# Transposed scores of two batches in one visit of four banks, in the last attention step of a fused cross-attention and gated feed-forward kernel

## The chip, the cores and the metric

The kernel runs on one core of one Trainium2 chip. The metric is the device time of one execution, in microseconds; lower is better. A core has a TensorE for matmuls (PE in the profile, with its weight loads as PEld), a VectorE (DVE), a ScalarE (ACT), a GpSimd (POOL) and a SyncE (SP), which issues most of the transfers. TensorE writes into PSUM; the kernel's four pools there have eight banks together, and a bank takes a tile of 128x512 numbers in f32.

## The reference

For each of 8 batches and 8 heads there are 512 tokens `x` and 32 state rows, of width 64. Tokens read the state, state rows read the tokens; the two results, put under each other (544 rows a batch, 512 columns), go through a gated feed-forward.

```python
scores = scale * np.matmul(x, state.transpose(0, 1, 3, 2))
a = exp(scores - scores.max(-1)); a /= a.sum(-1)
xread = np.matmul(a, state)
scores2 = scale * np.matmul(state, x.transpose(0, 1, 3, 2))   # the transposed scores
a2 = exp(scores2 - scores2.max(-1)); a2 /= a2.sum(-1)
sread = np.matmul(a2, x)
x2 = concatenate([xread, sread], axis=2)   # then heads side by side: 4352 x 512
out = ((1 / (1 + exp(-(x2 @ w_gate)))) * (x2 @ w_val)) @ w_out   # d_ff = 1536
```

## The kernel before

Everything is issued in an order written out by hand; each engine works through its own list in that order, and a scheduler adds the waits.

**Steps.** After a start written out call by call, a loop runs over `b` from 2 to 8. A step has 12 turns, `f` from 0 to 11, one for each 128 columns of `d_ff`. A turn does `gv_mm(b, f)`, the gate and value matmuls of the tokens of batch `b` (two PSUM tiles of the pool `GV`, which has two banks), `gv_th` (the tanh, on ACT), `gv_glu` (the product with the value, on DVE) and `out_mm(b - 1, f)`, four matmuls of the output of the batch before. In step 7 the output matmuls stand first in a turn. Turn by turn `out_mm` fills one bank (pool `OU`, one buffer), for four matmuls in each of three turns; in the third turn ACT copies the bank out (`res`, L318), and the next group's first matmul has to wait for that copy. Step 8 is the feed-forward of the state rows of all batches, which are gathered in `XS`; step 7 is the last step with attention in it.

**Transposed scores.** For one batch they go through these functions: `cT_mm` makes them in two PSUM banks (`e` = 0 and 1, each with four heads) with eight matmuls on 64x32 parts of TensorE, each 512 columns wide; `cT_max(b, e)` takes a maximum per row and scales it into the bias `nb` (DVE, L188 and L190); `cT_exp(b, e)` is the exponential with its sum (ACT, L196); `cT_nrm(b, e)` takes the reciprocal of the sum (DVE, L201) and multiplies by it on POOL (L204); `c_dma(b)` transposes the result through two transfers of SP's queue into the tile `Eb`; `sr_mm` multiplies it with the tokens (16 matmuls, 64 columns wide, L216); and `sr_cp` copies both halves of that into `XS` (ACT, then DVE, L221). Of the tiles `cE` (the exponentials), `nb` and `Eb` there are two buffers each.

**The last attention step.** Batches 0 and 1, whose feed-forward was done in the start, have their transposed scores only in step 7, beside the feed-forward of batch 7: `col(0, t)` in turns 0 to 4, `col(1, t)` in turns 3 to 7, `sr_mm` of batch 0 in turn 8, of batch 7 in turn 9 (its copies in turn 10), of batch 1 in turn 11. All of these take banks of the pool `SWP`, which has four; in step 7 nothing else uses it. The bank of the pool `AT` is idle in this step.

Of the kernel before, what the change touches and what calls it, by code (L numbers as in the profile page):

```python
# [16 lines left out]
def kernel(  # L17
# [14 lines left out]
    nc = tc.nc  # L32
    B, H, S, D = x.shape
# [30 lines left out]
    AT, OU, GV, SWP = (p_at, "at"), (p_out, "outp"), (p_gv, "gv"), (p_sw, "swp")  # L64
    xfs, xbs, xTs = {}, {}, {}
    Es, E1s, Ebs, abs_, aTs, SWs, glus = {}, {}, {}, {}, {}, {}, {}
    vec, act, pool = nc.vector.tensor_copy, nc.scalar.copy, nc.gpsimd.tensor_copy
# [42 lines left out]
    def at_xT_dma(b):  # L110
        xT = xT_tile(b)
        for c in range(4):
            nc.sync.dma_start_transpose(xT[:, :, c], xbs[b][:, c].rearrange("p h d -> p (h d)"))

    def S_mm(b, i, place, jjs=(0, 1)):
        if jjs[0] == 0:
            held["S", b, i] = place[0].tile((128, 4, 2, 2, Ns), FP, name="Sp", tag=place[1])
        ps = held["S", b, i]
        for jj in jjs:
            for c in range(4):  # L120
                nc.tensor.matmul(ps[:, c, :, jj], xTs[b][:, 2 * i + jj, c], sTz[:, b, 2 * i + jj], start=True, stop=True)  # L121

    def S_max(b, i):

        if b not in E1s:
            E1s[b] = ap_.tile((128, 4, 2, 4, Ns), FP, name="E1")
        ps = held["S", b, i].rearrange("p c e j n -> p (c e) j n")
        mx = held["mx", b, i] = ap_.tile((128, 8, 2), FP, name="mx")
        nc.vector.tensor_reduce(mx, ps, AX.X, ALU.max)  # L129

    def S_sub(b, i):

        mx, ps = held["mx", b, i], held["S", b, i].rearrange("p c e j n -> p (c e) j n")
        nc.vector.tensor_tensor(halfE(b, i), ps, mx.unsqueeze(3).to_broadcast((128, 8, 2, Ns)), ALU.subtract)  # L134

    def S_exp(b, i):
        nc.scalar.activation(halfE(b, i), halfE(b, i), AF.Exp, scale=scale)  # L137
# [4 lines left out]
    def n_sum(b, i):  # L142
        rs = ap_.tile((128, 8, 2), FP, name="rs")
        nc.vector.tensor_reduce(rs, halfE(b, i), AX.X, ALU.add)  # L144
        ri = held["ri", b, i] = ap_.tile((128, 8, 2), FP, name="ri")
        nc.vector.reciprocal(ri, rs)  # L146

    def n_mul(b, i, eng, lo=0, n=4):
        if b not in abs_:
            abs_[b] = ap_.tile((128, 4, 2, 128), BF, name="ab")  # L150
        ri, ce = held["ri", b, i], slice(2 * lo, 2 * lo + 2 * n)
        eng.tensor_tensor(abs_[b].rearrange("p c e (j n) -> p (c e) j n", n=Ns)[:, ce, 2 * i:2 * i + 2],  # L152
                          halfE(b, i)[:, ce], ri[:, ce].unsqueeze(3).to_broadcast((128, 2 * n, 2, Ns)), ALU.mult)
# [17 lines left out]
    def aT_dma(b):  # L171
        for c in range(4):
            nc.sync.dma_start_transpose(aT_tile(b)[:, c], abs_[b][:, c].rearrange("p e k -> p (e k)"))

    def cT_mm(b, places):

        pss = [p[0].tile((128, 512), FP, name="cTp", tag=p[1]) for p in places]
        for j in range(4):
            for e in range(2):
                rows = slice(e * 64, (e + 1) * 64)  # L180
                nc.tensor.matmul(pss[e][j * Ns:(j + 1) * Ns], sTz[rows, b, j, e],  # L181
                                 xTs[b][rows, j].rearrange("p c t -> p (c t)"), start=True, stop=True)
        held["cT", b] = pss

    def cT_max(b, e):

        mx = ap_.tile((128, 1), FP, name="cm")
        nc.vector.tensor_reduce(mx, held["cT", b][e], AX.X, ALU.max)  # L188
        nb = held["nb", b, e] = ap_.tile((128, 1), FP, name="nb")
        nc.vector.tensor_scalar(nb, mx, -scale, None, op0=ALU.mult)  # L190

    def cT_exp(b, e):

        ex = held["cE", b, e] = ap_.tile((128, 512), FP, name="cE")
        cs = held["cs", b, e] = ap_.tile((128, 1), FP, name="cs")
        nc.scalar.activation(ex, held["cT", b][e], AF.Exp, bias=held["nb", b, e], scale=scale, accum_out=cs)  # L196

    def cT_nrm(b, e, eng):

        rc = ap_.tile((128, 1), FP, name="rc")  # L200
        nc.vector.reciprocal(rc, held["cs", b, e])  # L201
        if ("cN", b) not in held:
            held["cN", b] = ap_.tile((128, 2, 512), BF, name="cN")
        eng.tensor_scalar(held["cN", b][:, e], held["cE", b, e], rc, None, op0=ALU.mult)  # L204

    def c_dma(b):
        Ebs[b] = ap_.tile((128, 4, 2, 128), BF, name="Eb")
        for e in range(2):
            nc.sync.dma_start_transpose(Ebs[b][:, :, e], held["cN", b][:, e])

    def sr_mm(b, place):
        sr = held["sr", b] = place[0].tile((128, 4, 2, Ns), FP, name="srp", tag=place[1])
        Eb = Ebs[b].rearrange("p c e (j n) -> p c e j n", n=Ns)
        for j in range(4):
            for c in range(4):
                nc.tensor.matmul(sr[:, j], xbs[b][:, c, 2 * j:2 * j + 2].rearrange("p h d -> p (h d)"),  # L216
                                 Eb[:, c, :, j], start=(c == 0), stop=(c == 3))

    def sr_cp(b, e, cp):
        rows = slice(e * 64, (e + 1) * 64)  # L220
        cp(XS[rows, :, b * Ns:(b + 1) * Ns], held["sr", b][rows, :, e])  # L221
# [46 lines left out]
    def sw_cp(b, lo, w, e, cp):  # L268
        cp(*sw_left.pop((b, lo, w, e)))  # L269
# [115 lines left out]
    def col(b, t):  # L385

        if t == 0:
            cT_mm(b, (AT, SWP) if b > 1 else (SWP, SWP))
            cT_max(b, 0)
        elif t == 1:  # L390
            cT_max(b, 1)
            cT_exp(b, 0)
        elif t == 2:
            cT_exp(b, 1)
        elif t == 3:
            cT_nrm(b, 0, nc.gpsimd)
        else:
            cT_nrm(b, 1, nc.gpsimd)
            c_dma(b)

    def row(b, t):

        if t == 0:
            S_mm(b, 0, AT)
            S_max(b, 0)
        elif t == 1:
            S_sub(b, 0)
            S_mm(b, 1, SWP)
            S_max(b, 1)
        elif t == 2:  # L410
            S_sub(b, 1)
            S_exp(b, 0)
        elif t == 3:
            S_exp(b, 1)
            n_sum(b, 0)
            n_mul(b, 0, nc.gpsimd)
        elif t == 4:
            n_sum(b, 1)
            n_mul(b, 1, nc.gpsimd)
        else:  # L420
            aT_dma(b)
# [274 lines left out]
    for b in range(2, B + 1):  # L696
        nb = b + 1 if b + 1 < B else None
        for f in range(NF):

            v, q = divmod(f, 6)  # L700
            if nb is not None and q == 0:
                sw_wide(nb, v)
                sw_cp(nb, v, 0, 0, act)
                sw_cp(nb, v, 0, 1, act)
            ahead = nb is not None and q == 0
            for first in (ahead, not ahead):
                if first:
                    gv_mm(b, f, SWP if b == B and f % 2 else GV)
                    gv_th(b, f)
                    gv_glu(b, f)  # L710
                elif b < B or f < 9:
                    out_mm(b - 1, f)
            if nb is not None:
                if q == 0:
                    sw_cp(nb, v, 1, 0, vec)
                if q in (1, 3, 4):
                    k = max(q + 1, 3)
                    sw_cp(nb, v, k // 2, k % 2, act)
                if f == 10:
                    sr_cp(b, 0, act)  # L720
                    sr_cp(b, 1, vec)
                if 0 <= f - (b < 4) < 6:
                    row(nb, f - (b < 4))
                elif f >= 7:
                    col(nb, f - 7)
                if f == (6 if b > 3 else 3) and nb + 2 < B:
                    load_x(nb + 2, nc.sync, 4 if nb + 3 == B else 1)
                if f == (1 if b > 2 else 6) and nb + 1 < B:
                    cast_x(nb + 1, pool, 0, 4)
                    cast_x(nb + 1, pool, 4, 4)  # L730
                    at_xT_dma(nb + 1)
            if b < B and f == 9:
                sr_mm(b, SWP)
            if b == B - 1:
                if f == 10:
                    sr_cp(b, 0, act)
                    sr_cp(b, 1, vec)
                for k in range(2):
                    if 0 <= f - 3 * k < 5:
                        col(k, f - 3 * k)  # L740
                    elif f == 8 + 3 * k:
                        sr_mm(k, SWP)
                        sr_cp(k, 0, act)
                        sr_cp(k, 1, vec)
    for k in range(6):
        out_mm(B, k)
    out_last(B - 1, 3)
# [30 lines left out]
```

## Time and profile before

| | |
|---|---|
| median of 3 runs | 230.65 us (230.24 to 230.70) |
| the profiled execution | 230.65 us, of which the profile's span is 228.9 us |
| clock that TensorE was granted | 1.0 of full speed |
| busy, share of the span | PE 96%, ACT 63%, DVE 60%, POOL 31% |
| chain that ended last, by engine | PE 84%, DMA 7%, ACT 2%, POOL 2% |
| step 7, from its first output matmul to the first of step 8 | 176.16 to 199.55 us |

The span is cut by instructions: each row of the timeline gives a start, a duration, the engine, the line, what is written from what, and in brackets the idle time before it and what ended it. Durations of pipelined instructions overlap: four matmuls of 512 columns show 1.03 us, but the next group starts 0.86 us after them. In this text "tanh of turn 3" and the like are those of step 7.

### The profile page before, as it was taken

The numbers are of one execution on the slowest core, as the hardware profiler recorded it, in microseconds if no ns is written. First come the engines' busy times: TensorE is split into PE (matmuls) and PEld (weight loads), VectorE is DVE, ScalarE is ACT, GpSimd is POOL, SyncE is SP. The second block draws the span as 40 slices with busy tenths as digits, with TensorE's granted clock in tenths as the row PEclk, the third lists the DMA queues.
The fourth block names the chain that finished last, engine by engine and source line by source line (L and its number), as shares of the span: only waits on it lengthen the run. The fifth ranks groups of instructions, "written<-read, shape, count | busy, mean of one in ns | idle before, by whom it ended". The sixth has DMA issues, their size and how long they took to land.

```text
span 228.9 us, 5007 instructions
## 1 busy us (share of the span) xinstructions
PE 219.1 (96%) x1885; PEld 111.5 (49%) x1911; DVE 138.0 (60%) x266; ACT 143.1 (63%) x288; POOL 71.4 (31%) x77
## 2 busy tenths in 40 slices
PE   8868999999999999999999999999999999999994
PEld 7653444434444444444444444445444434566744
DVE  0889779766587557666766577648755664422311
ACT  3588787677575866676767767584857655422411
POOL 3986371240507080307130533031301355000001
PEclk9999999999999999999999999999999999999999
DMA  6999979935794374842443766313121312411114
GB/s 215 269 201 285 206 88 182 269 85 126 209 292 134 61 181 94 246 148 74 92 126 83 238 84 142 89 46 87 57 46 75 99 37 69 116 39 77 46 26 115
DMA packets 47271, 29.49 MB, mean 129 GB/s; under 512 B 29872, under 2 KB 42544, under 8 KB 47248
## 3 DMA queue, kind: packets, MB, share of 16 engines
q1 hardware_dynamic: 40096, 21.84, 36.5%
q0 software_dynamic: 6864, 7.14, 17.0%
q8 instruction: 15, 0.25, 0.4%
q10 hardware_dynamic: 288, 0.20, 0.3%
q14 instruction: 8, 0.07, 0.1%
HBM read 18.35 MB, written 8.91 MB: 119 GB/s over the span
## 4 chain that ended last, share of the span: by engine, by line
PE 84%; DMA 7%; ACT 2%; issue 2%; POOL 2%; SPq 1%; DVE 0%; ACTq 0%
PE outp L314 36%; PE gvp L283 34%; PE swp L231 5%; PE gvp L286 5%; DMA wg<-in_moe_w_gate_dram 4%; DMA xf<-in_x_dram 2%; PE srp L216 2%; PE Sp L121 1%; SPq L74 1%; PE outp L334 1%; PE cTp L181 1%; POOL cN L204 1%; ACT res L318 1%; POOL xb L91 1%; ACT SW L269 1%
## 5 line engine op out<-in xcount | busy, mean ns | idle before, releaser
L298 DVE SCALAR_TENSOR_TENSOR glu<-th,gvp 128x512 bf16<-128x512 f32 (+1 forms) x108 | 70.3, 656 | 69.1 <-ACT th L293 52.8
L314 PE MATMUL outp<-wo,glu 128*128 128x512 bf16 x370 | 95.5, 379 | 1.7 <-issue 0.3
L283 PE MATMUL gvp<-aT,SW 128*128 128x512 bf16 x384 | 96.6, 379 | 0.3 <-DVE aT L169 0.3
L293 ACT ACTIVATE th<-gvp 128x512 f32<-128x512 f32 (+1 forms) x108 | 61.8, 576 | 51.2 <-PE gvp L283 41.4
L283 PEld LDWEIGHTS <-SW 128*128 128x128 bf16 x384 | 36.3, 98 | 44.8 <-issue 3.1
L314 PEld LDWEIGHTS <-glu 128*128 128x128 bf16 x396 | 36.5, 98 | 40.8 <-issue 3.2
L204 POOL TENSOR_SCALAR cN<-cE,rc 128x512 bf16<-128x512 f32 x16 | 24.9, 1564 | 66.2 <-DVE rc L201 53.4
L269 ACT CAST SW<-swp 128x512 bf16<-128x512 f32 x74 | 41.0, 586 | 3.5 <-PE swp L231 2.5
L152 POOL TENSOR_TENSOR ab<-E,ri 128x512 bf16<-128x512 f32 x16 | 16.7, 1047 | 48.4 <-DVE ri L146 21.7
L318 ACT ACTIVATE res<-outp 128x512 f32<-128x512 f32 x33 | 19.7, 597 | 16.8 <-PE outp L314 16.6
L269 DVE CAST SW<-swp 128x512 bf16<-128x512 f32 x22 | 14.7, 681 | 1.0 <-PE swp L231 1.0
L91 POOL CAST xb<-xf 128x1024 bf16<-128x1024 f32 (+1 forms) x14 | 13.6, 986 | 4.9 <-DMA xf<-in_x_dram 4.9
L196 ACT ACTIVATE cE<-cTp,nb 128x512 f32<-128x512 f32 x16 | 11.1, 694 | 0.8 <-POOL cN L204 0.8
L144 DVE TENSOR_REDUCE rs<-E 128x16 f32<-128x512 f32 x16 | 10.8, 675 | 0.7 <-ACT E L137 0.7
L188 DVE TENSOR_REDUCE cm<-cTp 128x1 f32<-128x512 f32 x16 | 10.9, 682 | 0.4 <-PE cTp L181 0.4
L137 ACT ACTIVATE E<-E 128x512 f32<-128x512 f32 x16 | 10.1, 637 | 1.6 <-DVE E L134 1.6
L129 DVE TENSOR_REDUCE mx<-Sp 128x16 f32<-128x512 f32 x16 | 10.7, 674 | 0.4 <-PE Sp L121 0.4
L134 DVE TENSOR_TENSOR E<-Sp,mx 128x512 f32<-128x512 f32 x16 | 10.9, 684 | 0.1
L325 POOL DMA_DIRECT2D out_dram<-res x2 | 1.1, 550 | 30.1 <-ACT res L318 30.1
L231 PE MATMUL swp<-wg,sTc 64*32 64x512 bf16 (+1 forms) x192 | 8.4, 328 | 0.2
L348 PE MATMUL warm<-ones 128*128 128x128 bf16 x87 | 7.6, 256 | 1.0 <-DVE ones L429 1.0
L231 PEld LDWEIGHTS <-sTc 64*32 64x32 bf16 x384 | 4.8, 91 | 7.4 <-issue 4.7
(62 smaller groups left out, 134.2 us busy)
## 6 DMA issues: line engine op xcount, KB each, us to landing
out_dram<-res SPq DMA_DIRECT2D x31, 256.0 KB, 2.4
xf<-in_x_dram SPq DMA_DIRECT2D x12, 256.0 KB, 4.8
xf<-in_x_dram SPq DMA_DIRECT2D x3, 1024.0 KB, 6.3
wo<-in_moe_w_out_dram POOLq DMA_DIRECT2D x3, 512.0 KB, 8.9
wv<-in_moe_w_val_dram POOLq DMA_DIRECT2D x2, 512.0 KB, 9.1
wg<-in_moe_w_gate_dram POOLq DMA_DIRECT2D x2, 512.0 KB, 10.1
xf<-in_x_dram POOLq DMA_DIRECT2D x2, 512.0 KB, 8.0
xf<-in_x_dram POOLq DMA_DIRECT2D x1, 1024.0 KB, 12.8
```

Of the source, the lines that this page charges most:

```text
L91: cp(xbs[b].rearrange("p c h d -> p h c d")[:, lo:lo + n], xfs[b][:, lo:lo + n])
L152: eng.tensor_tensor(abs_[b].rearrange("p c e (j n) -> p (c e) j n", n=Ns)[:, ce, 2 * i:2 * i + 2], halfE(b, i)[:, ce], ri[:, ce].unsqueeze ...
L196: nc.scalar.activation(ex, held["cT", b][e], AF.Exp, bias=held["nb", b, e], scale=scale, accum_out=cs)
L204: eng.tensor_scalar(held["cN", b][:, e], held["cE", b, e], rc, None, op0=ALU.mult)
L231: nc.tensor.matmul(pss[e][j * Ns:(j + 1) * Ns, o:o + n], sTc[rows, b, j] if b > 1 else sTz[rows, b, j, e], (wg, wv)[w][rows, j, lo:lo + n] ...
L269: cp(*sw_left.pop((b, lo, w, e)))
L283: nc.tensor.matmul(ps, SWs[b][:, g, w, fs], aTs[b][:, :, g], start=(g == 0), stop=(g == 1))
L286: nc.tensor.matmul(ps, (wg, wv)[w][:, j, fs], XS[:, j], start=(j == 0), stop=(j == 3))
L293: nc.scalar.activation(th, held["gv", b, f][0], AF.Tanh, scale=0.5)
L298: nc.vector.scalar_tensor_tensor(glus[b][:, f], held["th", b, f], 1.0, held["gv", b, f][1], ALU.add, ALU.mult)
L314: nc.tensor.matmul(ops[b, c], glus[b][:, f, c * 128:(c + 1) * 128], wo[:, f], start=(f == 0), stop=(f == NF - 1))
L318: nc.scalar.activation(res, ops[b, c], AF.Copy, scale=0.5)
```

## The change

The steps of batches 0 and 1 in step 7 get a table of their own, `first01(f)`, in place of the two shifted calls of `col`. Eight matmuls of batch 0 and eight of batch 1 follow each other in turn 0, into all four banks of `SWP`. The second exponential of batch 0 moves from turn 2 to turn 3, the second of batch 1 from turn 5 to turn 6; the maxima of batch 1 move from turns 3 and 4 to turns 2 and 3. In turn 3 the second maximum of batch 1 stands ahead of batch 0's first reciprocal. `sr_mm` of batch 7 moves from turn 9 to turn 4, that of batch 0 from turn 8 to turn 9; all three in this step use the bank of `AT`, and their copies follow them at once.

```diff
+    def sr_all(b, place):
+        sr_mm(b, place)
+        sr_cp(b, 0, act)
+        sr_cp(b, 1, vec)
+
+    def first01(f):
+
+        if f == 0:
+            for k in range(2):
+                cT_mm(k, (SWP, SWP))
+            cT_max(0, 0)
+        elif f == 1:
+            cT_max(0, 1)
+            cT_exp(0, 0)
+        elif f == 2:
+            cT_max(1, 0)
+        elif f == 3:
+            cT_max(1, 1)
+            cT_exp(0, 1)
+            cT_nrm(0, 0, nc.gpsimd)
+        elif f == 4:
+            cT_exp(1, 0)
+            cT_nrm(0, 1, nc.gpsimd)
+            c_dma(0)
+            sr_all(B - 1, AT)
+        elif f == 6:
+            cT_exp(1, 1)
+            cT_nrm(1, 0, nc.gpsimd)
+        elif f == 7:
+            cT_nrm(1, 1, nc.gpsimd)
+            c_dma(1)
+        elif f in (9, 11):
+            sr_all(f // 2 - 4, AT)
...
-            if b < B and f == 9:
+            if nb is not None and f == 9:
                 sr_mm(b, SWP)
             if b == B - 1:
-                if f == 10:
-                    sr_cp(b, 0, act)
-                    sr_cp(b, 1, vec)
-                for k in range(2):
-                    if 0 <= f - 3 * k < 5:
-                        col(k, f - 3 * k)
-                    elif f == 8 + 3 * k:
-                        sr_mm(k, SWP)
-                        sr_cp(k, 0, act)
-                        sr_cp(k, 1, vec)
+                first01(f)
```

## The prediction

> **What bounds the kernel now.** First the page: its span and its engines.
>
> ```profile
> span 228.9 us, 5007 instructions
> ## 1 busy us (share of the span) xinstructions
> PE 219.1 (96%) x1885; PEld 111.5 (49%) x1911; DVE 138.0 (60%) x266; ACT 143.1 (63%) x288; POOL 71.4 (31%) x77
> ```
>
> TensorE is busy for 96%. So an edit is worth what it takes from TensorE's list, or what it changes in the few places where TensorE waits for others. The second view is therefore the chain of work that ended last, in order of time, read in step 7: there is one stretch in it that isn't TensorE's.
>
> ```profile
> 183.34 0.61 ACT th L293
> 183.94 0.94 issue
> 184.88 1.57 POOL cN L204
> 186.50 0.56 issue
> 187.26 0.50 ACT res L318
> 187.80 1.02 PE outp L314 x4
> ```
>
> The third is the timeline of that stretch, engine by engine: start, duration, engine, line, what is written from what. PE:
>
> ```profile
> 183.60 0.41 PE L181 MATMUL cTp<-xT,sTz 64*32 64x512 bf16 x8
> 184.17 0.81 PE L314 MATMUL outp<-wo,glu 128*128 128x512 bf16 x3 [0.16 <-issue]
> 184.82 1.03 PE L283 MATMUL gvp<-aT,SW 128*128 128x512 bf16 x4
> 185.68 1.03 PE L314 MATMUL outp<-wo,glu 128*128 128x512 bf16 x4
> 186.54 1.03 PE L283 MATMUL gvp<-aT,SW 128*128 128x512 bf16 x4
> 187.80 1.02 PE L314 MATMUL outp<-wo,glu 128*128 128x512 bf16 x4 [0.23 <-ACT res L318]
> ```
>
> ACT:
>
> ```profile
> 182.10 0.68 ACT L196 ACTIVATE cE<-cTp,nb 128x512 f32<-128x512 f32 x1
> 182.67 0.20 ACT L196 ACTIVATION_READ_ACCUMULATOR cE<-cTp,nb 128x1 f32 x1
> 183.34 0.60 ACT L293 ACTIVATE th<-gvp 128x512 f32<-128x512 f32 x1 [0.46 <-PE gvp L283]
> 185.51 0.60 ACT L293 ACTIVATE th<-gvp 128x512 f32<-128x512 f32 x1 [1.58 <-PE gvp L283]
> 186.48 0.69 ACT L196 ACTIVATE cE<-cTp,nb 128x512 f32<-128x512 f32 x1 [0.37 <-POOL cN L204]
> 187.07 0.19 ACT L196 ACTIVATION_READ_ACCUMULATOR cE<-cTp,nb 128x1 f32 x1
> 187.16 0.59 ACT L318 ACTIVATE res<-outp 128x512 f32<-128x512 f32 x1
> 187.64 0.60 ACT L293 ACTIVATE th<-gvp 128x512 f32<-128x512 f32 x1
> ```
>
> DVE, and POOL's product:
>
> ```profile
> 183.97 0.69 DVE L298 SCALAR_TENSOR_TENSOR glu<-th,gvp 128x512 bf16<-128x512 f32 x1 [1.04 <-ACT th L293]
> 184.57 0.15 DVE L201 RECIPROCAL rc<-cs 128x1 f32<-128x1 f32 x1
> 184.64 0.67 DVE L188 TENSOR_REDUCE cm<-cTp 128x1 f32<-128x512 f32 x1
> 185.35 0.15 DVE L190 TENSOR_SCALAR nb<-cm 128x1 f32<-128x1 f32 x1
> ```
>
> ```profile
> 184.88 1.56 POOL L204 TENSOR_SCALAR cN<-cE,rc 128x512 bf16<-128x512 f32 x1 [5.52 <-ACT th L293]
> ```
>
> What to see: groups of four matmuls start 0.86 us apart (184.82, 185.68, 186.54). The group of turn 6 could start at 186.54 + 0.86 = 187.40 and starts at 187.80: a stall of 0.40 us. It waits for the bank that `res` empties. `res` stands in ACT's list behind batch 1's first exponential (186.48), and this waits for POOL's product of batch 0 (184.88 + 1.56 = 186.44), because there are two buffers of `cE` and it takes the one that the product reads. The product in turn waits for batch 0's reciprocal (184.57), right behind the product with the tanh of turn 3 on DVE. The first "issue" of the chain, 0.94 us, is these two on DVE. That is the path on which the change works, on every link.
>
> **The visit.** Turn 0's visit, on PE:
>
> ```profile
> 177.02 1.03 PE L283 MATMUL gvp<-aT,SW 128*128 128x512 bf16 x4
> 177.98 0.41 PE L181 MATMUL cTp<-xT,sTz 64*32 64x512 bf16 x8
> 178.32 1.04 PE L314 MATMUL outp<-wo,glu 128*128 128x512 bf16 x4
> ```
>
> It costs TensorE from 177.02 + 0.86 = 177.88 to 178.32, 0.44 us. Turn 3 has another; the group behind it has lost a record, but must have started at 184.82 - 0.86 = 183.96, 0.36 after the visit's first matmul, as in turn 0 (0.34). What a second group of eight costs in the same visit is not in step 7; the nearest rows are the first three groups of a visit of 32 matmuls of the same tile, in step 6.
>
> ```profile
> 152.39 0.41 PE L231 MATMUL swp<-wg,sTc 64*32 64x512 bf16 x8
> 152.62 0.40 PE L231 MATMUL swp<-wv,sTc 64*32 64x512 bf16 x8
> 152.83 0.29 PE L231 MATMUL swp<-wg,sTc 64*32 64x256 bf16 x8
> ```
>
> A second group of eight starts 0.23 us after the first, the third 0.21 after that. So eight more matmuls cost 0.22, and the other 0.22 of a visit is paid once for each visit. Two visits cost 0.88 now, one of 16 will cost 0.44 + 0.22 = 0.66: a gain of 0.22 us. Bounds: 0 (nothing is paid per visit) to 0.44 (the second group rides along for nothing). A rule of the Trainium skill speaks against this gain: by "TensorEngine Tiling (Array Packing)", section Performance Considerations (Instruction Overhead), a matmul has about 60 cycles of overhead, each one, and there are 16 matmuls before and after. By that rule the gain would be 0, and the rows above do not agree with it: groups inside a visit stand 0.22 apart. The same page's section Tiling Modes (Key Properties) says that a change of mode drains the array, and with that they agree.
>
> **Turn 0 to 3.** The maximum of batch 0 waits for its own eight matmuls and stands behind turn 0's product with the tanh as now, so nothing changes but that TensorE is 0.22 later from turn 1 on, and ACT and DVE with it. In turn 2 the exponential that leaves frees ACT, where nobody was kept waiting.
>
> **Turn 3 and 4, on DVE and ACT.** Now the order on DVE is product with the tanh, reciprocal. After the change it is that product, the second maximum of batch 1, its bias, the reciprocal. From the rows: product to next instruction 0.60 (183.97 to 184.57), maximum to bias 0.71 (184.64 to 185.35), bias to reciprocal about 0.08, as reciprocal to maximum (0.07). The reciprocal so comes 0.60 + 0.71 + 0.08 = 1.39 after the product instead of 0.60, 0.79 later. The bias gains a wait too: its buffer (one of two) is read by batch 0's second exponential, which has moved into turn 3. That one follows the tanh of turn 3 (183.34 + 0.22 + 0.60 = 184.16 at the latest) and takes 0.77 with the reading of its sum (182.10 to 182.87), so it ends by 184.93; the bias would start at 183.97 + 0.22 + 1.31 = 185.50. So this wait is hidden, with 0.57 us to spare, by the product with the tanh and the maximum; without that cover it would hold up the reciprocal one for one.
>
> POOL starts 0.31 after the reciprocal and takes 1.56, and the exponential follows 0.04 after it, as now. So batch 1's first exponential comes at 186.48 + 0.22 + 0.79 = 187.49. Behind it are queued, on ACT: the copy of batch 7's `srp` (new in turn 4), `res` of turn 5, the tanh of turn 5. The copy's price in such a place:
>
> ```profile
> 175.22 0.26 ACT L221 CAST XS<-srp 64x128 bf16<-64x128 f32 x1
> 175.49 0.60 ACT L318 ACTIVATE res<-outp 128x512 f32<-128x512 f32 x1
> ```
>
> 0.27 us. So `res` starts at 187.49 + 0.68 (186.48 to 187.16) + 0.27 = 188.44, and turn 6's first matmul 0.64 after it (187.16 to 187.80): 189.08.
>
> **What TensorE has until then.** Batch 7's `sr_mm` comes into turn 4. Its price (PE, batch 0's, with the group behind it), when SP issues the two transfers of its `Eb`, and how long all transfers into `Eb` take to land:
>
> ```profile
> 192.97 0.63 PE L216 MATMUL srp<-Eb,xb 128*128 128x64 bf16 x16
> 193.44 1.03 PE L314 MATMUL outp<-wo,glu 128*128 128x512 bf16 x3
> ```
>
> ```profile
> 177.85 2.73 SPq L209 DMA_TRANSPOSE Eb<-cN  x2
> ```
>
> ```profile
> DMA to landing us min/median/max: 2.4/2.4/5.4
> ```
>
> 0.47 us, moved and not added. The transfers are issued by 180.58, and 2.4 after that is 182.98, ahead of turn 4's end (about 185.45). TensorE would be ready for turn 6 at 187.40 + 0.22 (visit of turn 0 longer) - 0.44 (none in turn 3) + 0.47 = 187.65. The stall is then 189.08 - 187.65 = 1.43 instead of 0.40: 1.03 more.
>
> **Afterwards.** DVE's half of the `srp` copy waits for ACT's, with the product with the tanh of turn 5 queued behind it; that product waits anyway for a tanh that comes after `res` (at 188.44 + 0.48 and 0.60 long), so it costs nothing, and turn 6 stands to `res` as now. POOL's second product and the first two transfers of SP come about 0.4 to 1 us later, and `sr_mm` of batch 0 is a turn later. Batch 1's second exponential has its buffer when its turn comes. From 189.08 on turns are 2 x 0.86 = 1.73 long. Turn 7's gate matmuls start at 189.08 + 1.73 + 0.86 = 191.67; its tanh 0.69 later (184.82 to 185.51), the product with it 0.63 after that (183.34 to 183.97), the last reciprocal 0.60, POOL 0.31: 193.90, done at 195.46. The second transfer into batch 1's `Eb`, issued in some 1.4 (half of 2.73) and landed 2.4 later, is there by 199.3; `sr_mm` of turn 11 wants it at 189.08 + 6 x 1.73 + 0.47 = 199.93. SP's only work behind it is an output transfer. Step 8 starts with the same copies as now. The banks of `AT` and `SWP` change owners at no cost: both are free by then.
>
> **Sum.** -0.22 for the visit, +1.03 for the stall, +0.81 us on the profiled execution's 230.65 (a span of 228.9 with 1.75 around it), which is also the median of the runs. Forecast 231.46 us. Its own range: a gain of 0 to 0.44 in the visit and an added stall between 0.75 (reciprocal 0.6 later, the copy half hidden) and 1.3 (1.0 later): 230.65 - 0.44 + 0.75 = 230.96 to 230.65 + 1.30 = 231.95.
>
> **Rivals.**
>
> No gain in the visit: overhead is paid by the matmul and not by the visit. Time 230.65 + 1.03 = 231.68. Against it stand the groups inside a visit, 0.22 apart where a whole visit is 0.44. It is the rule of the Trainium skill's page "TensorEngine Tiling (Array Packing)" that was named above. Chance 0.10.
>
> The last transfer comes late: one landing took 5.4 where the median is 2.4. If the second transfer of batch 1, asked for at 195.46, lands after 5.4, at 200.86, `sr_mm` in turn 11 waits 0.93 and the time is 232.39. It decides from a landing of 4.5 on. The median is equal to the least, so the slow one is rare. Chance 0.05.
>
> Only the old stall stays: the reciprocal's delay is taken up on the way, because POOL's product ends earlier than its record says. 230.65 - 0.22 = 230.43. Against it: the exponential started 0.04 after the recorded end. Chance 0.09.
>
> Faster: the product is through before ACT gets to batch 1's first exponential, that is by the end of the tanh of turn 4 (185.51 + 0.22 + 0.60 = 186.33 at the latest, with the reciprocal at 184.4 or before, some 0.2 after the product with turn 3's tanh begins; DVE would have to do the reciprocal ahead of the product with the tanh). Then `res` follows its own matmuls, the old stall goes as well, and the time is 230.65 - 0.22 - 0.40 = 230.03. For it: all four banks are full by turn 0, so the data are there early. Against it: DVE works in order, and the maximum is ahead. Chance 0.08.
>
> **How the numbers follow.** The forecast has 0.68. About 0.2%, 0.46 us, is what a measurement of this kernel can tell from no change: slower means over 231.11. Of the forecast's 0.68 some 0.05 lie between 230.96 and 231.11; with the 0.09 that makes 0.14 for the same. Slower: 0.63 + 0.10 + 0.05 = 0.78. Faster 0.08. The range takes the forecast's own, 0.2 below it for the scatter of the runs (230.24 to 230.70), and above it half the way to the late transfer: 230.75 to 232.2, with the two good cases (0.17) left out.
>
> **What would show it.** Right: one visit of 16 in turn 0 taking 0.66; the reciprocal 1.4 behind turn 3's product with the tanh; batch 1's first exponential waiting on ACT from about 185.8 to 187.5 for POOL; the first matmul of turn 6 released by `res` after some 1.4 idle; no other new gap until step 8. Wrong: a stall there of 0.4 or less; a visit of 0.9; a wait for a transfer in turn 9 or 11.

## The result, and the profile after

| | before | changed |
|---|---|---|
| median (range), 11 runs each | 230.60 us (230.24 to 231.23) | 231.48 us (231.20 to 232.81) |
| ratio, 95% interval | | 1.0048 (1.0031 to 1.0066) |
| again, in a later set on one chip: 29 and 12 runs | 230.71 us | 231.32 us; 1.0024 (1.0001 to 1.0047) |
| step 7: first output matmul to first gate matmul of step 8, in the profile | 176.16 to 200.61: 24.45 us | 177.33 to 202.55: 25.22 us |

The changed kernel is slower, by 0.88 us in the medians of this set and 0.61 in the later one; 0.81 was forecast. (The ratios are worked out from all runs and not from the two medians, here and below.) The profiled execution of it was one of 232.81 us, above the median: it had lost 1.17 us ahead of step 7, where both kernels have the same instructions in the same order. Step 7 itself grew by 0.77. So times below are compared within step 7, and starts are 1.17 later throughout.

The visit, on PE (start, duration, line, what is written from what):

```profile
178.19 1.03 PE L283 MATMUL gvp<-aT,SW 128*128 128x512 bf16 x4
179.15 0.63 PE L181 MATMUL cTp<-xT,sTz 64*32 64x512 bf16 x16
179.71 1.04 PE L314 MATMUL outp<-wo,glu 128*128 128x512 bf16 x4
```

From 178.19 + 0.86 = 179.05 to 179.71: 0.66 us for 16 matmuls, where two visits of eight took 0.44 each. The gain of 0.22 is there. Then the stall, with PE's and ACT's rows:

```profile
187.09 1.03 PE L314 MATMUL outp<-wo,glu 128*128 128x512 bf16 x4
187.96 1.03 PE L283 MATMUL gvp<-aT,SW 128*128 128x512 bf16 x4
190.20 1.02 PE L314 MATMUL outp<-wo,glu 128*128 128x512 bf16 x4 [1.21 <-ACT res L318]
```

```profile
186.46 0.60 ACT L293 ACTIVATE th<-gvp 128x512 f32<-128x512 f32 x1 [0.46 <-PE gvp L283]
188.73 0.69 ACT L196 ACTIVATE cE<-cTp,nb 128x512 f32<-128x512 f32 x1 [1.68 <-POOL cN L204]
189.32 0.19 ACT L196 ACTIVATION_READ_ACCUMULATOR cE<-cTp,nb 128x1 f32 x1
189.41 0.24 ACT L221 CAST XS<-srp 64x128 bf16<-64x128 f32 x1
189.56 0.59 ACT L318 ACTIVATE res<-outp 128x512 f32<-128x512 f32 x1
```

TensorE was ready for turn 6 at 187.96 + 0.86 = 188.82 and began at 190.20: a stall of 1.38 us instead of 0.40. (The bracket counts idle time from the modelled end of the last matmul and says 1.21.) ACT sat idle for 1.68 at batch 1's first exponential and then had the copy and the exponential to do ahead of `res`. What held the exponential, on DVE and POOL:

```profile
185.36 0.69 DVE L298 SCALAR_TENSOR_TENSOR glu<-th,gvp 128x512 bf16<-128x512 f32 x1 [0.25 <-ACT th L293]
185.96 0.68 DVE L188 TENSOR_REDUCE cm<-cTp 128x1 f32<-128x512 f32 x1
186.75 0.15 DVE L190 TENSOR_SCALAR nb<-cm 128x1 f32<-128x1 f32 x1
186.83 0.15 DVE L201 RECIPROCAL rc<-cs 128x1 f32<-128x1 f32 x1
```

```profile
187.14 3.10 POOL L204 TENSOR_SCALAR cN<-cE,rc 128x512 bf16<-128x512 f32 x2 [6.60 <-ACT th L293]
```

The reciprocal comes 1.47 after the product with turn 3's tanh (0.60 before the change), because the second maximum of batch 1 and its bias are ahead of it. POOL's product follows 0.31 later (the row merges two of 1.56 each), ends at 188.70, and the exponential starts at 188.73. The waits of step 7 in total, summed by who waited for whom (time, times, longest), show no other wait of TensorE's matmuls for another engine; these are the two rows that matter here:

```profile
ACT cE L196 <- POOL cN L204: 1.7, 1, 1.7
PE outp L314 <- ACT res L318: 1.2, 1, 1.2
```

### The profile page after: what moved, and what is told of

Same layout as the page of the kernel before. It is cut to its first block, busy times and chain, and to the rows that moved or that the text cites. A ratio compares the mean times of both kernels' runs of the same rounds, so it can differ in the third digit from the quotient of the medians.

```text
span 230.8 us, 5006 instructions
## 1 busy us (share of the span) xinstructions
PE 219.3 (95%) x1885; PEld 111.2 (48%) x1911; DVE 138.3 (60%) x266; ACT 142.9 (62%) x288; POOL 71.2 (31%) x77
## 4 chain that ended last, share of the span: by engine, by line
PE 85%; DMA 5%; ACT 3%; POOL 2%; issue 2%; DVE 2%; ACTq 0%; DVEq 0%
PE outp L314 36%; PE gvp L283 34%; PE swp L231 5%; PE gvp L286 5%; DMA wg<-in_moe_w_gate_dram 4%; DMA xf<-in_x_dram 2%; PE srp L216 1%; ACT SW L269 1%; PE Sp L121 1%; PE outp L334 1%; PE cTp L181 1%; POOL cN L204 1%; ACT res L318 1%; DVE glu L298 1%; ACT E L137 0%
```

## The experiments

The theory, "queue theory" in the expectations: the exponential waits for a buffer that POOL's product holds, the product waits for a reciprocal that has been put behind other work, and the whole of ACT's list, `res` with it, stands behind the exponential. Rivals: that the four banks filled at once, or the single bank for three batches, slow down those who read them; and that it is `sr_mm` of batch 7 and its copies in turn 4 that delay `res`. Each kernel was run 11 or 12 times, beside runs of the kernel before on the same chip.

| | step 7, expected by the queue theory | step 7, measured | kernel, against before (95%) |
|---|---|---|---|
| changed, four buffers of `cE` | 23.83 | 176.15 to 199.99: 23.84 | 230.14 against 230.70: 0.9971 (0.9954 to 0.9988) |
| changed, reciprocal first | 24.35 | 176.25 to 200.60: 24.35 | 230.88 against 230.70: 1.0008 (0.9989 to 1.0026) |
| changed, `sr_mm` of batch 7 in turn 5 | 24.95 to 25.1 | 175.85 to 200.91: 25.06 | 231.31 against 230.70: 1.0022 (0.9999 to 1.0046) |
| before, one visit alone | 24.67 | 178.01 to 202.68: 24.67 | 230.96 against 230.70: 1.0021 (0.9997 to 1.0045) |
| before, four buffers of `cE` | 24.05 | 177.54 to 201.61: 24.07 | 230.53 against 230.62: 0.9982 (0.9963 to 1.0001) |
| changed, four buffers, rest a turn earlier | 23.64 | 176.20 to 199.84: 23.64 | 229.97 against 230.62: 0.9978 (0.9957 to 0.9999) |
| changed, two visits | 25.44 | 177.04 to 202.48: 25.44 | 232.34 against 230.62: 1.0066 (1.0044 to 1.0088) |

**Four buffers of `cE`.**

```diff
-        ex = held["cE", b, e] = ap_.tile((128, 512), FP, name="cE")
+        ex = held["cE", b, e] = ap_.tile((128, 512), FP, name="cE", bufs=4)
```

> The changed kernel with four buffers of cE in place of two, so that batch 1's first exponential takes a buffer that POOL's product does not read. Measured on step 7, from its first output matmul to the first gate matmul of step 8 (24.45 us before, 25.22 after the change). Queue theory (ACT stands at the exponential until POOL's product is through, and res is queued behind it): the exponential follows the tanh of turn 4 at once, res follows its matmuls, the stall ahead of turn 6 is gone (0 to 0.1), step 7 takes 24.45 - 0.40 - 0.22 = 23.83, the kernel 0.6 less than before, about 230.0. Bank rival (four banks filled at once, or the one bank of AT shared by three batches, slow the readers): the stall stays at 1.4 and step 7 at 25.2. Copy rival (the sr_mm of batch 7 and its copies in turn 4 delay res): the stall stays over 1, step 7 about 25.

ACT, then PE, in its profile:

```profile
185.28 0.60 ACT L293 ACTIVATE th<-gvp 128x512 f32<-128x512 f32 x1 [0.46 <-PE gvp L283]
185.90 0.69 ACT L196 ACTIVATE cE<-cTp,nb 128x512 f32<-128x512 f32 x1
186.48 0.19 ACT L196 ACTIVATION_READ_ACCUMULATOR cE<-cTp,nb 128x1 f32 x1
186.57 0.24 ACT L221 CAST XS<-srp 64x128 bf16<-64x128 f32 x1
186.98 0.60 ACT L318 ACTIVATE res<-outp 128x512 f32<-128x512 f32 x1 [0.16 <-PE outp L314]
```

```profile
186.78 1.03 PE L283 MATMUL gvp<-aT,SW 128*128 128x512 bf16 x4
187.64 1.03 PE L314 MATMUL outp<-wo,glu 128*128 128x512 bf16 x4
```

The exponential goes 0.62 after the tanh starts, `res` now waits for its own matmuls (0.16) and not for an exponential ahead of it, and turn 6 starts 0.86 after turn 5's gate group: no stall. There is next to no room, though. Where TensorE waits for `res`, its next group starts 0.64 after `res` does (189.56 to 190.20 in the changed kernel); here, without a wait, it starts 0.66 after it (186.98 to 187.64). So `res` can be only 0.02 later before TensorE pays for it, which is why each delay on ACT came through almost in full. The four banks, the single bank and the copies of batch 7 are as in the changed kernel; the cost is gone with the buffer alone. That rules out both rivals as the main cause.

**Reciprocal first.** The line of `cT_nrm` in turn 3 is moved up:

```diff
         elif f == 3:
+            cT_nrm(0, 0, nc.gpsimd)
             cT_max(1, 1)
             cT_exp(0, 1)
-            cT_nrm(0, 0, nc.gpsimd)
```

> The changed kernel with batch 0's first reciprocal and product put ahead of batch 1's second maximum in turn 3, nothing else. Queue theory: the reciprocal is 0.60 behind the product with turn 3's tanh, as before the change, and batch 1's first exponential 0.79 to 0.87 earlier than in the changed kernel; res is behind it and behind the srp copy; the stall ahead of turn 6 falls from 1.38 to about 0.5, step 7 takes 24.35, the kernel 0.1 less than before (no change that can be told). Bank rival and copy rival: nothing that they name is changed, so the stall stays at 1.4 and step 7 at 25.2.

DVE, then PE:

```profile
184.28 0.69 DVE L298 SCALAR_TENSOR_TENSOR glu<-th,gvp 128x512 bf16<-128x512 f32 x1 [0.25 <-ACT th L293]
184.88 0.15 DVE L201 RECIPROCAL rc<-cs 128x1 f32<-128x1 f32 x1
```

```profile
186.88 1.03 PE L283 MATMUL gvp<-aT,SW 128*128 128x512 bf16 x4
188.26 1.02 PE L314 MATMUL outp<-wo,glu 128*128 128x512 bf16 x4 [0.36 <-ACT res L318]
```

The reciprocal is 0.60 behind again and the stall is 188.26 - 187.74 = 0.52. Two instructions fewer ahead of it on DVE make step 7 shorter by 0.87 us: the position of one 0.15 us instruction carries the result. The kernel's own time can't be told from before, as expected.

**`sr_mm` of batch 7 in turn 5.**

```diff
             c_dma(0)
+        elif f == 5:
             sr_all(B - 1, AT)
```

> The changed kernel with sr_mm of batch 7 and its copies in turn 5 in place of turn 4, so that the copy stands behind res on ACT. TensorE has the same work ahead of turn 6. Queue theory: only the copy's place ahead of res goes, 0.15 (what it took in the profile after) to 0.27; the stall ahead of turn 6 is 1.1 to 1.25, step 7 takes 24.95 to 25.1. Copy rival: the stall falls to about 0.4 and step 7 to 24.2. Bank rival: 25.2.

```profile
187.25 0.69 ACT L196 ACTIVATE cE<-cTp,nb 128x512 f32<-128x512 f32 x1 [1.68 <-POOL cN L204]
187.84 0.19 ACT L196 ACTIVATION_READ_ACCUMULATOR cE<-cTp,nb 128x1 f32 x1
187.93 0.59 ACT L318 ACTIVATE res<-outp 128x512 f32<-128x512 f32 x1
```

These are ACT's rows. `res` follows the exponential at once, and step 7 is 0.16 shorter. So the copy in that place cost 0.15 to 0.16, and the exponential still waits 1.68 for POOL.

**One visit alone, in the kernel before.** `col` makes both batches' scores when batch 0's turn comes:

```diff
         if t == 0:
-            cT_mm(b, (AT, SWP) if b > 1 else (SWP, SWP))
+            if b > 1:
+                cT_mm(b, (AT, SWP))
+            elif b == 0:
+                cT_mm(0, (SWP, SWP))
+                cT_mm(1, (SWP, SWP))
```

> The kernel before with the one visit alone: batch 1's eight matmuls in turn 0 behind batch 0's, all else in the turns where it was. Plain view (a visit less is 0.22 less): step 7 takes 24.23, the kernel 0.2 less than before. Queue theory: the visit is longer by 0.22 in turn 0, and what ACT, DVE and POOL do up to batch 1's first exponential comes 0.22 later, so the bank that turn 6 waits for comes 0.22 later; the visit saved in turn 3 (0.44) only lets TensorE wait longer. The stall is 0.40 + 0.44 = 0.84, step 7 takes 24.67, the kernel 0.2 more than before.

```profile
188.17 1.03 PE L283 MATMUL gvp<-aT,SW 128*128 128x512 bf16 x4
189.87 1.02 PE L314 MATMUL outp<-wo,glu 128*128 128x512 bf16 x4 [0.67 <-ACT res L318]
```

The stall is 189.87 - 189.03 = 0.84 and step 7 is 0.22 longer than before: the part of the change that saves TensorE 0.22 costs 0.22 as long as the stall is there. The kernel's own ratio isn't clear of 1; the length of step 7 in the trace is what decides.

**Four buffers of `cE` in the kernel before.** The same one-line edit.

> The kernel before with four buffers of cE, nothing else. Queue theory: the stall of 0.40 ahead of turn 6 goes, step 7 takes 24.45 - 0.40 = 24.05, the kernel 0.4 less than before; what the changed kernel with four buffers had beyond this (23.84) is then the one visit less, 0.21. Rival (the stall of before has another cause than the buffer): 24.45.

```profile
187.93 1.03 PE L283 MATMUL gvp<-aT,SW 128*128 128x512 bf16 x4
188.79 1.03 PE L314 MATMUL outp<-wo,glu 128*128 128x512 bf16 x4
```

The old stall is gone as well, at 24.07. Against the 23.84 of the changed kernel with four buffers that leaves 0.23, the size of the visit; the other moves of the change take no work from TensorE. Without the stall the saving comes through in full. The kernel's own ratio is not clear of 1 here either.

**Everything behind the exponentials a turn earlier.** On top of the four buffers:

```diff
-        elif f == 6:
+        elif f == 5:
             cT_exp(1, 1)
             cT_nrm(1, 0, nc.gpsimd)
-        elif f == 7:
+        elif f == 6:
             cT_nrm(1, 1, nc.gpsimd)
             c_dma(1)
-        elif f in (9, 11):
+        elif f in (8, 10):
             sr_all(f // 2 - 4, AT)
```

> The changed kernel with four buffers of cE and what follows moved forward by a turn: batch 1's second exponential and first product to turn 5, second product and transfers to turn 6, sr_mm of batch 0 to turn 8, of batch 1 to turn 10. Queue theory: no stall ahead of turn 6, and the first gate matmul of step 8 no longer waits for the copies of batch 1 (it started 0.19 to 0.20 after TensorE was ready): step 7 takes 23.84 - 0.20 = 23.64, the kernel 0.8 less than before. Rival (the transfers of batch 1 land too late for turn 10): TensorE waits ahead of turn 10's sr_mm, and the 0.20 is lost again or more.

```profile
198.98 1.03 PE L314 MATMUL outp<-wo,glu 128*128 128x512 bf16 x4
199.84 0.60 PE L286 MATMUL gvp<-XS,wg 128*128 128x256 bf16 x4
```

In the kernel before, the same two groups are

```profile
199.55 1.03 PE L314 MATMUL outp<-wo,glu 128*128 128x512 bf16 x3
200.61 0.60 PE L286 MATMUL gvp<-XS,wg 128*128 128x256 bf16 x4
```

that is 1.06 apart. With the earlier turns, step 8's first gate matmul starts 0.86 after the output group, without the wait of 0.20, and step 7 is at 23.64.

**Two visits in the changed kernel.**

```diff
         if f == 0:
-            for k in range(2):
-                cT_mm(k, (SWP, SWP))
+            cT_mm(0, (SWP, SWP))
             cT_max(0, 0)
...
         elif f == 2:
+            cT_mm(1, (SWP, SWP))
             cT_max(1, 0)
```

> The changed kernel with batch 1's eight matmuls in a visit of their own, at the end of turn 2 ahead of its first maximum; all else as changed. Queue theory: turn 0 is 0.22 shorter, turn 2 is 0.44 longer, so everything from turn 3 on is 0.22 later, with the same stall of 1.4 ahead of turn 6: step 7 takes 25.44. Bank rival (four banks in one visit slow the readers): the stall becomes smaller and step 7 takes less than 25.2.

```profile
187.90 1.03 PE L283 MATMUL gvp<-aT,SW 128*128 128x512 bf16 x4
190.13 1.02 PE L314 MATMUL outp<-wo,glu 128*128 128x512 bf16 x4 [1.21 <-ACT res L318]
```

The stall is the same 1.37 with two banks filled at a time as with four, and step 7 is 0.22 longer. How many banks are filled at a time plays no part. The kernel as a whole, however, was 1.72 over before where step 7 is 0.99 over.

**Again, three of them on one chip,** for that and for the best version.

> The changed kernel again, on the same chip as the two that follow. Step 7 should take 25.22 us as in its first profile; the stretch ahead of step 7, where its instructions are those of before, took 177.33 us there and 176.16 before. If that 1.2 is scatter of the start, this profile has another value and the median is 0.8 to 0.9 over before; if the start belongs to the program, the value comes again.

> The changed kernel with two visits again. Its step 7 took 25.44 us, 0.99 over before, but its median was 1.7 over before; the stretch ahead of step 7 took 177.04 with a TensorE clock of 0.85 from 10 to 20 us. If the 0.7 is scatter of that start on one chip, the median here is about 1.0 over before; if it belongs to the program, about 1.7 again.

> The version with four buffers of cE and everything behind the exponentials a turn earlier, again. Step 7 23.64 us, 0.81 less than before; the kernel 0.6 to 0.8 less than before, 1.5 to 1.6 less than the changed kernel on the same chip.

Step 7 came out at 25.21, 25.43 and 23.65 us; the medians at 231.32, 232.15 and 230.67 us against 230.71 of before, ratios 1.0024 (1.0001 to 1.0047), 1.0061 (1.0036 to 1.0086) and 0.9990 (0.9963 to 1.0017). The stretch ahead of step 7 took 175.88, 176.46 and 177.13. In the changed kernel it was 1.45 shorter than in its first profile, so that was scatter. In the kernel with two visits a surplus over step 7 came again, smaller: 1.44 over before where step 7 is 0.98 over. The rows of two stretches, first from the changed kernel and then from the one with two visits (window, length, busy time of PE, PEld, DVE, ACT, POOL, then the clock that TensorE was granted, the share of the DMA engines and GB/s):

```profile
16.00:18.00 2.00, 1.66 (x44) 0.82 (x39) 1.38 (x3) 2.00 (x5) 2.00 (x3) 1.00 1.27 203
18.00:20.00 2.00, 2.00 (x20) 0.85 (x18) 1.90 (x5) 1.70 (x4) 0.77 (x2) 1.00 1.26 209
```

```profile
16.00:18.00 2.00, 1.98 (x43) 0.99 (x43) 1.30 (x3) 1.92 (x4) 2.00 (x3) 0.60 1.27 203
18.00:20.00 2.00, 2.00 (x12) 1.10 (x10) 1.90 (x5) 1.17 (x3) 0.76 (x2) 0.55 1.29 220
```

The 0.60 and 0.55 are means over stretches that the low clock only partly fills. Cut at its edges, the same profile shows half the clock for 3.4 us:

```profile
16.40:19.80 3.40, 3.40 (x43) 1.82 (x39) 3.00 (x7) 2.77 (x6) 2.16 (x4) 0.50 1.27 204
```

That is 1.7 us of full clock lost, 0.7% of the span of 230.2, and so it shows as a mean clock of about 0.993 for the whole execution. Of the kernel with two visits, 10 of the 12 executions have a mean clock of 0.992 or 0.993 here, and 7 of 11 had one of 0.993 or less in its first set; the two at about 1.0 here are the two shortest (231.56 and 231.58). The other kernels have such executions too: 1 of 12 and 3 of 11 of the changed kernel, 9 of 29, 6 of 28 and 17 of 35 of before, 2 to 7 of 12 of the others. In every one of these sets the executions with a mean clock of at least 0.998 have the lower median. Against before's executions of that kind, the changed kernel's are 0.81 longer here, those with four buffers 0.58 shorter, and those with two visits 1.07 longer here (two executions) and 1.38 in the first set (four). So the low clock goes with most of the surplus in this set, but not in the first. Why the kernel with two visits meets the low clock so often, with the same instructions up to step 7, and what the rest of its surplus is, stays open.

The version with the four buffers and the earlier turns is the shortest in step 7, 0.81 below before and 1.56 to 1.58 below the changed kernel. In the kernel's time that was 0.65 below before on one chip. On the other the expectation of 0.6 to 0.8 less than before, and 1.5 to 1.6 less than the changed kernel, was missed: it was 0.04 below before, not to be told from it, and 0.65 below the changed kernel. Its profile there shows a slower start (177.13) at full clock; what made it slower is not known. The changed kernel with four buffers of `cE` alone is clear of 1: 0.9971 (0.9954 to 0.9988).

## Why the prediction was right

It was right in sign, size and mechanism: the reciprocal late on DVE, the exponential held by POOL's product, `res` queued behind the exponential, and TensorE waiting for the bank.

| step | predicted | measured |
|---|---|---|
| visit of 16 | 0.66 us, a gain of 0.22 | 0.66; a gain of 0.22 to 0.23 in pairs of kernels |
| reciprocal behind the product with the tanh | 1.39 | 1.47 |
| reciprocal, through POOL's product, to the exponential | 0.31 + 1.56 + 0.04 | 186.83 to 188.73: 1.90 |
| copy of `srp` ahead of `res` | 0.27 | 0.15 |
| stall ahead of turn 6 | 1.43 | 1.38 |
| step 7 | +0.81 | +0.77 |
| transfers, step 8, other turns | nothing | no new gap; the wait of 0.20 ahead of step 8 as before |

Two terms were off, in opposite ways, and it is luck that they nearly cancel (0.12 too much and 0.08 too little). How close the kernel's medians came is in part luck as well: they differ by 0.88 in one set and by 0.61 in the other. The copy was priced from a place where it stood behind another copy (0.27 to the next instruction); behind the reading of a sum it took 0.15 (189.41 to 189.56). And the reciprocal was 0.08 later than said: the bias came 0.79 after the start of the maximum where 0.71 was taken. Batch 0's second exponential had ended by 185.99 (185.22 with its sum read from 185.79 for 0.20), well before 186.75, so the wait was hidden as claimed. An extra of 0.06 is there too where that exponential had ended before the maximum began (184.96 to 185.73, with the reciprocal first; there the sum was read by 184.91), and none in the bias of turn 2 (184.24 to 184.96, 0.72), whose buffer had been free for longer. That it is the added wait itself which takes the time was not tested.

The bounds of the added stall are a little off by the prediction's own terms: a reciprocal 0.6 later with half the copy gives 0.70 and not 0.75, one 1.0 later gives 1.24 and not 1.3. The measured 0.98 lies inside either way. The forecast also puts 1.4 of issuing ahead of the last transfer into `Eb`. It was issued at 196.6, when its product was done (195.03 and 1.56 long), and landed 2.4 after that, at 199.0, some 2 us ahead of the `sr_mm` that needs it (201.02).

The rival by the overhead rule of the Trainium skill's page "TensorEngine Tiling (Array Packing)", section Performance Considerations (Instruction Overhead), falls: 16 matmuls in one visit took 0.66 and in two 0.88, so what is saved belongs to the visit. The late transfer did not occur: all landings into `Eb` in step 7 took 2.4. The rival with only the old stall had POOL's product end earlier than its record says; the exponential started 0.03 after the recorded end (188.70 to 188.73), and the stall was 1.38. The faster rival had the product through by the end of turn 4's tanh (186.46 + 0.60 = 187.06); it was through at 188.70. The times that these two gave were reached only by edits: with the reciprocal first, step 7 is at 24.35 with a stall of 0.52, near the old one of 0.40, and with four buffers of `cE` it is at 23.84, as the faster rival had it (24.45 - 0.22 - 0.40 = 23.83), though the product itself is no earlier there.

## What to carry to other kernels

A saving on the busiest engine counts only where that engine isn't about to wait: here 0.22 us of TensorE time turned into 0.22 us of loss until the wait behind it was taken away. Before two chains are interleaved, follow for each shared buffer who frees it, and where that one's own inputs stand in their queues; an engine that works through its list in order and waits for a buffer holds up everything queued behind it, the bank copy for TensorE included. A second pair of buffers for the waiting tile was worth more than the reordering: 0.38 of step 7 in the kernel before (24.45 to 24.07), and the reordering another 0.23 on top.

## What was not expected of the hardware

The stretch ahead of step 7 varies by up to 2.2 us between profiles (175.85 to 178.01) with the same instructions, which is nearly three times the effect that was to be measured. So the experiments are told apart by the length of step 7, which came to within 0.02 us of what was expected, or into the range that was given, in all of them. In four of the twelve profiles TensorE's clock was at 0.50 for 3.4 us in the start, somewhere between 15 and 21 us. That is not all of the scatter: the profiles without it still range from 175.85 to 177.54. The Trainium skill, "TensorE: Matmul & The Clock Gate" (Part 1), describes a clock that is halved after an idle window of about 3.4 us, with windows that run free of the kernel's start. The 0.50 and the 3.4 us agree with that, and so would a start that scatters. No run here shows the windows or what set the low clock off: in the profile of the kernel with two visits, TensorE's longest wait between 8 and 17 us is 1.6 us, shorter than such a window.
